# A recurrence with a mixer behind it on one core: another scan, mixer steps kept in PSUM, other buffers, and the order of all work written out as a list

## The chip, the cores and the metric

The kernel runs as one launch on one core of a Trainium2 chip. The metric is device microseconds (us) from start to end. The median of three runs of the kernel before is 1073.24 us (1073.01 to 1075.44). The profile is that of one further execution, read by engine: TensorE (PE, its weight loads PEld), VectorE (DVE), ScalarE (ACT), GpSimd (POOL), and SyncE (SP), which issues the DMAs.

## The reference

Two parts follow each other. The first is a linear recurrence over 768 tokens, for 4 batches x 8 heads with a state of 40 x 40:

```python
for t in range(S):                                   # S = 768
    y[:, :, t] = einsum('bhd,bhde->bhe', rt, state)
    Sa = einsum('bhde,bhe->bhd', state, at)
    state = state * wt[:, :, None, :] - einsum('bhd,bhe->bhde', Sa, bt) + einsum('bhd,bhe->bhde', vt, kt)
```

Its output, as rows of 320 values for each token, goes through a mixer:

```python
gate = 1 / (1 + exp(-gate_pre))                      # gate_pre: 5 taps of a causal convolution over tokens
x = (gate * (x @ w_val)) @ w_out                     # 320 x 320 each
xk, xr = mu_k*x + (1-mu_k)*x_prev, mu_r*x + (1-mu_r)*x_prev
k = maximum(xk @ w_k, 0);  v = (k*k) @ w_v           # 320 x 1024, 1024 x 320
out = 1 / (1 + exp(-(xr @ w_r))) * v
```

## The kernel before, in words

**The recurrence** (class `Attn`) goes through 24 chunks of 32 tokens. The decays are made into running products by scans on DVE, forward (`fwd`, L281) and backward (`bwd`, L294). The reciprocal of a chunk's total product (L284) times the forward products gives `ys` (POOL, L288). PE multiplies the scaled vectors among themselves (`gram`, L322), DVE masks the result (`gmask`, L326), and it is written to a scratch array in DRAM and read back with the 32 x 32 triangles of the (batch, head) pairs over all partitions. There the triangles are inverted, row after row, on DVE (`inv`, L368, L373, L376): in seven waves of chunks, (0,1), (2,3), (4 to 7), and so on; in the last five waves POOL takes rows 22 to 32 of each. The inverses go through DRAM to the layout `tr` of the steps.

The step of a chunk is a chain through the state: `yi` (PE, L443) reads the state `s0`; `gmm` (L458), `umm` (L471) and `fmm` (L492) follow, with a copy on ACT behind each of `yi`, `gmm` and `umm` and a masking on POOL (`cut`, L484); then `scl` (DVE, L501) scales the new state, `trn` turns it round on PE (L515, a transpose, and L516, a matmul with the identity, eight times each) and `trc` (ACT, L519) copies it to `s0` for the next chunk. The 32 pairs are handled as two groups, `gr` 0 and 1, so one block of `trn` stands for one chunk and one group: 46 blocks. The loads `wa`, `zt` and `vrt` of a step have one buffer each.

**The mixer** (class `Moe`) runs in 12 units of 64 tokens of each batch, 256 columns; unit u can begin when chunk 2u+1 is written out. Its steps are: load `X`; five taps on DVE (`tap`, L1007 the first, L1009 the others); sigmoid; the split of an operand into a high part (ACT, L805) and a low part (POOL, L809 and L811); the matmuls `val`, `out`, `k` (all in `fm`, L831), `r` (L883) and `v` (`vmm`, L891), three products for each pair of parts; and behind the `k` matmul `kpost`: relu (L870), which reads PSUM and frees its bank, square (L872), the high part (L874) and the low part (DVE, L876). The steps between matmuls lie in SBUF.

**PSUM** has eight banks, four for the recurrence (`pa`) and four for the mixer (`pm`). A task that begins a result takes a bank, and the last task that reads it gives it back.

**What sets the order.** Everything is a task with an engine, a cost, the tasks it needs, and a target time. `Plan.order` plays the tasks against a model of the engines and gives each engine its order; the kernel is then issued in it. Each engine works off its instructions strictly in that order.

The weights come as 64-bit words and are turned into two parts by seven small steps for each piece (`wconv`, L739 to L753).

Of the kernel before, what the change touches and what calls it, by code (L numbers as in the profile page):

```python
# [18 lines left out]
L = 32  # L19
# [29 lines left out]
F32_MIN_HI = 3.4332275390625e-05
PACE = 1.12  # L50
BURST = 3
ACC = [535.94, 4640.39]
GAP = 2.23
LAT = 170.0
DMA_RATE = 330.0
WAIT = {"p": 107.21, "v": 0, "a": 449.76, "g": 84.62, "d": 0.0}
WINDOW = 4096 / 1.2
COLUMNS = {"gram": 160, "ztr": 200, "rv": 160, "yi": 320, "gmm": 864, "umm": 288, "fmm": 1152, "trn": 200,
           "val": 2048, "out": 2048, "kmm": 2048, "rmm": 2560, "vmm": 1920}
WARM = 3072  # L60
# [14 lines left out]
class Task:  # L75
    def __init__(self, eng, cost, fn, deps, prio, bank, frees, nbytes, seq):
        self.eng, self.cost, self.fn, self.deps, self.prio = eng, cost, fn, deps, prio
        self.bank, self.frees, self.nbytes, self.seq = bank, frees, nbytes, seq
        self.left, self.ready, self.users = 0, 0.0, []


class Plan:
    """Puts the work of all engines in order by a model of their times: a task starts when the
    tasks it names are over and its engine is free; the one with the lowest priority number first."""

    def __init__(self):
        self.tasks, self.names, self.held, self.log = {}, set(), {}, []

    def add(self, name, eng, cost, fn, deps=(), prio=0.0, bank=None, frees=None, nbytes=0):
        assert name not in self.tasks, name  # L90
        prio += SHIFT.get(name[0], 0.0)
        self.tasks[name] = Task(eng, cost, fn, list(deps), prio, bank, frees, nbytes, len(self.tasks))
        self.names.add(name[0])

    def order(self):
# [1001 lines left out]
```

## Time and profile before

| | us |
|---|---|
| median of three runs | 1073.24 |
| the profiled execution, span | 1072.7 |
| PE busy in it | 823.6 (77%) |
| DVE busy | 610.5 (57%) |
| ACT busy | 465.3 (43%) |
| POOL busy | 375.1 (35%) |

Three stages can be told apart. Up to 294.0 us the first chunks are prepared and the weights converted, until the first `vmm` of unit 0 runs (at 293.50). From 294.0 to 981.0 recurrence and mixer run side by side; it ends when the last `fmm` does. From 981.0 to the end only the mixer is left. Busy times are sums of durations on one engine. The granted clock is the share of its full speed that TensorE was allowed; here it stands at 1.00 or at 0.50, and an average between the two means a mix of both.

### The profile page before, as it was taken

How to read it: one execution, taken by the hardware profiler on the slowest of the kernel's cores; microseconds unless marked ns; L12 is line 12 of the kernel's file. 1: busy time of each engine (PE TensorE's matmuls, PEld its weight loads, DVE VectorE, ACT ScalarE, POOL GpSimd, SP SyncE). 2: the span in 40 equal slices, each digit the busy share in tenths (PEclk: the TensorE clock that was granted, in tenths of full speed). 3: DMA queues.
4: the chain of work that ended last, by engine and by line, in shares of the span. 5: the costliest groups of instructions: out<-in, count | busy, mean ns of one | idle time of the engine just before them, and what ended most of it. 6: DMA issues, size and time to landing. Idle time of an engine off the chain costs nothing.

```text
span 1072.7 us, 33076 instructions
## 1 busy us (share of the span) xinstructions
PE 823.6 (77%) x14096; PEld 699.6 (65%) x14096; DVE 610.5 (57%) x1331; ACT 465.3 (43%) x1185; POOL 375.1 (35%) x477
## 2 busy tenths in 40 slices
PE   3222213864798868997998998796989999999998
PEld 2122112644676757887777877585868888889998
DVE  6546847837934783347686347855258525125662
ACT  6312213423523443354435532443355565456665
POOL 3433533334513442245331434323033123024431
PEclk9999999856768676588677775776878898679999
DMA  5453443551236314354135452234431433211101
GB/s 164 143 153 135 145 113 114 161 128 62 64 79 143 97 51 125 81 113 121 49 78 136 119 128 81 77 106 103 94 83 50 120 76 90 63 50 39 27 13 25
DMA packets 145903, 101.82 MB, mean 95 GB/s; under 512 B 120156, under 2 KB 123228, under 8 KB 143868
## 3 DMA queue, kind: packets, MB, share of 16 engines
q1 hardware_dynamic: 145756, 99.70, 35.1%
q8 instruction: 111, 1.82, 0.7%
q14 instruction: 36, 0.29, 0.1%
HBM read 66.64 MB, written 33.03 MB: 93 GB/s over the span
## 4 chain that ended last, share of the span: by engine, by line
PE 47%; DMA 20%; DVE 19%; SPq 6%; issue 3%; ACT 3%; POOL 1%; DVEq 0%; POOLq 0%; ACTq 0%
PE pm L831 13%; PE pa L516 7%; PE pm L891 7%; DMA d<-in_fd_dram 6%; SPq L246 6%; PE pa L515 5%; PE pa L492 4%; PE pa L443 3%; DMA X<-xs 3%; DVE tn L376 3%; DMA buf<-in_w_k_dram 3%; DVE buf L1009 3%; DVE tmv L373 3%; PE pm L883 2%; PE pa L458 2%
## 5 line engine op out<-in xcount | busy, mean ns | idle before, releaser
L484 POOL TENSOR_TENSOR mt<-mt,mask 64x512 f32<-64x512 f32 x48 | 65.1, 1358 | 154.0 <-ACT mt L479 44.1
L515 PE MATMUL pa<-ident,mt 40*40 40x40 f32 x368 | 83.6, 227 | 38.7 <-DVE sg L326 12.9
L516 PE MATMUL pa<-ident,mt 40*40 40x40 f32 x736 | 111.0, 241 | 0.4
L335 PE MATMUL pa<-ident,d 104*128 104x104 f32 x192 | 36.3, 334 | 94.7 <-POOL d L307 42.5
L492 PE MATMUL pa<-mt,zt 128*40 128x72 f32 x1536 | 78.1, 265 | 26.2 <-POOL mt L484 13.1
L831 PE MATMUL pm<-hh,whk 128*128 128x256 f32 x288 | 94.1, 332 | 1.7 <-POOL hh L811 1.3
L376 DVE TENSOR_TENSOR tn<-tn,tmv 128x240 f32<-128x240 f32 (+22 forms) x204 | 91.4, 448 | 4.5
L373 DVE TENSOR_TENSOR tmv<-tn,al 128x240 f32<-128x240 f32 (+22 forms) x204 | 89.7, 440 | 4.6
L335 PEld LDWEIGHTS pa<-ident,d 104*128 104x128 f32 x192 | 25.6, 185 | 100.5 <-POOL d L307 59.2
L492 PEld LDWEIGHTS pa<-mt,zt 128*40 128x40 f32 x1536 | 64.9, 141 | 36.3 <-POOL mt L484 15.4
L501 DVE TENSOR_TENSOR mt<-pa,cl 40x160 f32<-40x160 f32 x184 | 58.8, 319 | 51.1 <-PE pa L492 40.9
L831 PE MATMUL pm<-hh,wlk 128*128 128x256 f32 x288 | 87.2, 308 | 0.0
L479 ACT COPY mt<-pa 32x288 f32<-32x288 f32 x192 | 74.8, 390 | 27.9 <-PE pa L471 22.9
L307 POOL TENSOR_TENSOR d<-d,tl 104x512 f32<-104x512 f32 x42 | 62.7, 1499 | 56.1 <-DVE tl L294 39.3
L515 PEld LDWEIGHTS pa<-ident,mt 40*40 40x40 f32 x368 | 36.3, 99 | 65.7 <-DVE sg L326 13.7
L516 PEld LDWEIGHTS pa<-ident,mt 40*40 40x40 f32 x736 | 63.1, 128 | 22.7 <-DVE mt L501 1.1
L519 ACT COPY s<-pa 104x320 f32<-104x320 f32 x46 | 19.6, 426 | 132.2 <-PE pa L516 121.8
L876 DVE TENSOR_TENSOR kl<-buf,kh 128x512 fp32r<-128x512 f32 x48 | 37.5, 780 | 67.5 <-ACT kh L874 67.4
L322 PE MATMUL pa<-ya,d 40*32 40x32 f32 x3072 | 48.1, 223 | 32.8 <-ACT sz L339 11.5
L891 PE MATMUL pm<-whv,kh 128*128 128x320 f32 x192 | 72.4, 377 | 0.5 <-DVE buf L935 0.5
L322 PEld LDWEIGHTS pa<-ya,d 40*32 40x32 f32 x3072 | 41.0, 135 | 42.2 <-issue 15.3
L891 PE MATMUL pm<-whv,kl 128*128 128x320 f32 x192 | 65.8, 343 | 1.1 <-DVE kl L876 1.0
(128 smaller groups left out, 2175.8 us busy)
## 6 DMA issues: line engine op xcount, KB each, us to landing
d<-in_fd_dram SPq DMA_DIRECT2D x46, 322.8 KB
vrt<-in_vr_dram SPq DMA_DIRECT2D x48, 160.0 KB
slya<-ya SPq DMA_DIRECT2D x48, 160.0 KB
slab<-sz SPq DMA_DIRECT2D x24, 320.0 KB
zt<-slab SPq DMA_DIRECT2D x24, 320.0 KB
slab<-sg SPq DMA_DIRECT2D x24, 256.0 KB
mt<-in_vt_dram SPq DMA_DIRECT2D x48, 80.0 KB
ysj<-slya SPq DMA_DIRECT2D x48, 80.0 KB
```

The costliest lines, as they stand in the source:

```text
L246: self.nc.sync.dma_start(out, in_)
L307: e.tensor_mul(kb, kb, t3.unsqueeze(2).to_broadcast([104, 8, 2, L]))
L322: self.nc.tensor.matmul(ps[32 * q:32 * q + 32, i * L:(i + 1) * L], lhsT=kb[r:r + 40, m, o:o + L], rhs=ah[r:r + 40, m, :], start=True, stop ...
L373: eng.tensor_mul(t3, tn[:, lo:hi, k:k + 1].to_broadcast([128, ns, nt]), al[:, k:k + 1, k + 1:L].to_broadcast([128, ns, nt]))
L376: eng.tensor_add(tn[:, lo:hi, k + 1:L], tn[:, lo:hi, k + 1:L], t3)
L479: self.nc.scalar.copy(self.mv(gr)[96:128, 4 * mh:4 * mh + 4, par, :], ps[32 * q:32 * q + 32, 0:288].rearrange("p (m x) -> p m x", x=72))
L484: self.nc.gpsimd.tensor_mul(mm, mm, self.mask[64:128].unsqueeze(1).to_broadcast([64, 16, L]))
L492: self.nc.tensor.matmul(ps[r:r + 40, k * 72:k * 72 + 72], lhsT=self.zt[:, zof(mof(gr, i)) + par, :], rhs=self.mt[gr][:, 2 * i + par, :], s ...
L515: self.nc.tensor.transpose(ps[0:40, n], x[:, 0], one)
L516: self.nc.tensor.matmul(ps[64:104, n], lhsT=x[:, 1], rhs=one, start=True, stop=True)
L831: self.nc.tensor.matmul(ps[0:n, (mt % 2) * NT:(mt % 2) * NT + NT], lhsT=ww[:, mt * 128:mt * 128 + n], rhs=xx, start=(i == 0), stop=(i == l ...
L891: self.nc.tensor.matmul(ps[:, 0:DM], lhsT=xx[:, k, sl], rhs=ww, start=(k == 0 and i == 0), stop=(k == 7 and i == 2))
```

## The change

- **Seeded scan.** The backward scan comes first. The reciprocal of its totals is written into `seed`, and the forward scan starts from it, so that it gives `ys` at once: the POOL multiplication (L288) and the DVE copy of the totals (L285) go, and a small copy on ACT (`clc`) comes.
- **Mixer steps in PSUM.** The taps are added up in a PSUM bank, the first of them on ACT; the gate's product goes back into `val`'s bank, and its low part is taken on DVE from there; `mixadd` reads `out`'s bank; relu and square work in place in `k`'s bank until the low part has been read. The bits of the weight conversion lie in a PSUM bank too, its low part moves from POOL to DVE, and it has four buffers instead of three.
- **Scratch.** One array of 64 x 2304 for each chunk becomes two of 128 rows, `slg` and `slz`. The padding rows of `d` are set once by memsets instead of DMAs.
- **Inverses.** The rows of waves 0 and 1 are issued in blocks of eight, with one other DVE instruction among those of wave 0; all rows of the later waves are on DVE.
- **Double buffers** for `wa`, `zt` and `vrt`: a load waits for the step two chunks back.
- **trn** has no transpose any more: sixteen matmuls with the identity for a block.
- **Order.** `Plan.run` plays a fixed list of 3362 task numbers and a list of banks; there is no model in the kernel.

The diff, cut to what is spoken of (line numbers of the code after are given with the rows of its order below):

```diff
@@ Plan
+        order = [int(i) for line in ORDER for i in line.split()]
+        for i in order:
+            t = self.tasks[names[i]]
+            if t.bank and t.bank not in self.held:
+                self.held[t.bank] = int(next(banks))
+            t.fn()
...
@@ Attn: preparation
-    def fwd(self, c):
-        nc, n = self.nc, NM * (L + 1) + 1
-        nc.vector.tensor_tensor_scan(
-            self.ct[:, 0:n], self.d[c % 2][:, 0:n], self.rst[:, 0:n], 0.0, ALU.mult, ALU.add)
-        cl = self.cl[c % 12]
-        nc.vector.reciprocal(cl[:, 1, :], self.ct3()[:, :, L])
-        nc.vector.tensor_copy(cl[:, 0, :], self.ct3()[:, :, L])
-    def ys(self, c):
-        self.nc.gpsimd.tensor_mul(
...
+        nc.vector.reciprocal(self.seed[:, 0:YS:L + 1], self.total())
+    def clc(self, c):
+        self.nc.scalar.copy(self.cl[c % 12], self.total())
+    def fwd(self, c):
+        self.nc.vector.tensor_tensor_scan(self.ya[c % 2][:, 0:YS], self.d[c % 2][:, 0:YS], self.seed, 0.0,
+                                          ALU.mult, ALU.add)
...
@@ Attn: inverses
-SPLIT = [(("v", 0, 16),), (("v", 0, 16),)] + [(("v", 0, 22), ("g", 22, 32))] * 5
+SPLIT = [(("v", 0, 16),), (("v", 0, 16),)] + [(("v", 0, 32),)] * 5
+BLOCK = [8, 8] + [1] * 5
...
@@ Attn: step
-            [(n, c - 1, g) for n in ("rv", "yi") for g in range(2)], b - 0.9, nbytes=328e3)
+            [(n, c - 2, g) for n in ("rv", "yi") for g in range(2)], b - 0.9)
...
     def trn(self, c, gr):
         ps = self.bank("trn", c, gr)
         for i in range(8):
             x, n, one = self.mt[gr][0:40, 2 * i:2 * i + 2, 0:40], slice(i * D, i * D + D), self.ident[0:40, 0:40]
-            self.nc.tensor.transpose(ps[0:40, n], x[:, 0], one)
-            self.nc.tensor.matmul(ps[64:104, n], lhsT=x[:, 1], rhs=one, start=True, stop=True)
+            for par in range(2):
+                self.nc.tensor.matmul(ps[64 * par:64 * par + 40, n], lhsT=x[:, par], rhs=one, start=True, stop=True)
...
@@ Moe
-            nc.gpsimd.tensor_sub(p[4][0:n], bf[0:n], p[3][0:n])
+            nc.vector.tensor_sub(p[4], bf, p[3])
...
-        kr = self.kr[j % 2]
+        kr = self.bank("k", u, j).rearrange("p (k n) -> p k n", n=NT)
         if step == 0:
-            nc.scalar.activation(kr, self.bank("k", u, j).rearrange("p (k n) -> p k n", n=NT), AF.Relu)
+            nc.scalar.activation(kr, kr, AF.Relu)
...
-                add(("tap", u, k, t), "v", 396 if t else 266, lambda k=k, t=t: self.tapf(gt, k, t),
+                add(("tap", u, k, t), "v" if t else "a", 400 if t else 300, lambda k=k, t=t: self.tapf(u, k, t),
...
-            nc.vector.tensor_mul(gflat()[0:n, k], gflat()[0:n, k],
-                                 ps[0:n, 0:(2 - h) * NT].rearrange("p (k n) -> p k n", n=NT))
+            nc.vector.tensor_mul(ps, gflat()[0:n, k], ps)
...
+ORDER = [
...
+    "0 1826 7 487 6 27 3 1824 900 1841 1849 8 868 10 13 9 1833 12 1827 864 21 28 23 29 24 1842 11 5 31 19 33 34 30 16",
...
+]
```

Where the first step of the recurrence stands on PE before (the step of chunk 0, group 0; `mt` with the lower number is group 0, `x8` folds equal neighbours):

```order
L471 MATMUL pa_126<-gs_115,tr 32x72 x16
L322 MATMUL pa_124<-ya_103,d_87 32x32 x16
L471 MATMUL pa_126<-gs_116,tr 32x72 x16
L492 MATMUL pa_124<-mt_111,zt 40x72 x8
L492 MATMUL pa_126<-mt_111,zt 40x72 x8
L322 MATMUL pa_124<-ya_103,d_87 32x32 x16
L515 MATMUL pa_123<-ident,mt_111 40x40
L516 MATMUL pa_123<-ident,mt_111 40x40
L515 MATMUL pa_123<-ident,mt_111 40x40
L516 MATMUL pa_123<-ident,mt_111 40x40
```

The transpose L515 and the matmul L516 take turns, eight times each. The same place on PE now (L384 is `umm`, L405 `fmm`, L429 `trn`, L356 the `yi` of the next chunk):

```order
L384 MATMUL pa_132<-gs_123,tr 32x72 x16
L384 MATMUL pa_132<-gs_124,tr 32x72 x16
L405 MATMUL pa_132<-mt_119,zt_117 40x72 x16
L405 MATMUL pa_135<-mt_120,zt_117 40x72 x8
L429 MATMUL pa_132<-ident,mt_119 40x40 x16
L405 MATMUL pa_135<-mt_120,zt_117 40x72 x8
L356 MATMUL pa_132<-vrt_128,s_121 40x32 x16
L429 MATMUL pa_135<-ident,mt_120 40x40 x16
```

`trn` is one run of sixteen matmuls now. On DVE, among the inverses of wave 0, before (L373 and L376 are the inverse, L742 to L748 the weight conversion):

```order
L742 TENSOR_SCALAR buf<-buf 128x256
L373 TENSOR_TENSOR tmv<-tn,al 128x133
L744 SCALAR_TENSOR_TENSOR buf<-buf 128x256
L376 TENSOR_TENSOR tn<-tn,tmv 128x7x19
L746 SCALAR_TENSOR_TENSOR buf<-buf 128x256
L373 TENSOR_TENSOR tmv<-tn,al 128x126
L748 SCALAR_TENSOR_TENSOR buf<-buf 128x256
L376 TENSOR_TENSOR tn<-tn,tmv 128x7x18
```

61 other instructions of DVE lie among the 58 of wave 0, which end at DVE's 188th. Wave 0 on DVE now (L278, L283 and L286 are the inverse, L234 is `gmask`):

```order
L234 TENSOR_TENSOR sg<-pa_135,gm 128x2x128
L278 SCALAR_TENSOR_TENSOR tn<-al,tn 128x31
L278 SCALAR_TENSOR_TENSOR tn<-al,tn 128x30
L278 SCALAR_TENSOR_TENSOR tn<-al,tn 128x29 x2
L278 SCALAR_TENSOR_TENSOR tn<-al,tn 128x28 x2
L283 TENSOR_TENSOR tmv<-tn,al 128x81
L286 TENSOR_TENSOR tn<-tn,tmv 128x3x27
L283 TENSOR_TENSOR tmv<-tn,al 128x78
L286 TENSOR_TENSOR tn<-tn,tmv 128x3x26
```

The 58 have one other among them and end at DVE's 119th. Of the whole of DVE, 414 instructions stood ahead of the first low part of `kpost` (L876) before, and 476 stand there now; DVE has 1333 against 1345 in all, POOL 482 against 302. On PE, around the last `fmm` of the recurrence, before:

```order
L831 MATMUL pm_221<-hh_212,whval 128x256
L831 MATMUL pm_221<-hh_212,wlval 128x256
L492 MATMUL pa_126<-mt_112,zt 40x72 x8
L492 MATMUL pa_124<-mt_112,zt 40x72 x8
L831 MATMUL pm_219<-hh_212,whval 64x256
L831 MATMUL pm_219<-hh_212,wlval 64x256
L831 MATMUL pm_219<-hl_213,whval 64x256
```

It stands among `val` matmuls of the mixer, with 640 mixer matmuls behind it. Now:

```order
L820 MATMUL pm_255<-whv,kh 128x320
L405 MATMUL pa_132<-mt_119,zt_118 40x72 x8
L405 MATMUL pa_135<-mt_119,zt_118 40x72 x8
L405 MATMUL pa_134<-mt_120,zt_118 40x72 x8
L405 MATMUL pa_133<-mt_120,zt_118 40x72 x8
L820 MATMUL pm_255<-whv,kh 128x320
L820 MATMUL pm_255<-wlv,kh 128x320
```

It stands among `vmm` matmuls (L820), and 504 mixer matmuls are behind it. The matmuls of PE are 8386 in both.

## Rows read from the trace of the kernel before

**Rows 1.** Stretches: window, its length, busy of PE, PEld, DVE, ACT, POOL; clock, DMA.
```profile
0.00:283.50 283.50, 112.35 (x2648) 92.03 (x2648) 190.15 (x413) 93.47 (x229) 116.20 (x136) 0.90 0.44 128
0.00:294.00 294.00, 118.69 (x2754) 96.87 (x2755) 199.53 (x434) 99.17 (x243) 118.85 (x137) 0.89 0.43 125
294.00:981.00 687.00, 620.16 (x10705) 519.65 (x10703) 366.92 (x820) 311.25 (x821) 226.39 (x296) 0.75 0.36 91
981.00:1072.70 91.70, 84.75 (x643) 83.12 (x640) 44.09 (x78) 54.85 (x122) 29.84 (x45) 1.00 0.10 24
```

**Rows 2.** The page's chain that ended last, share by engine.
```profile
PE 47%; DMA 20%; DVE 19%; SPq 6%; issue 3%; ACT 3%; POOL 1%; DVEq 0%; POOLq 0%; ACTq 0%
```

**Rows 3.** Stretches, line L515 alone: window, length, busy of PE, PEld; clock, DMA.
```profile
294.00:981.00 687.00, 73.68 (x328) 32.09 (x328) 0.75 0.36 91
```

**Rows 4.** Timeline of PE, 854 to 864: start us, us, engine, line, operation, tiles.
```profile
853.77 1.20 PE L492 MATMUL pa<-mt,zt 128*40 128x72 f32 x32
854.90 0.80 PE L443 MATMUL pa<-vrt,s 40*40 40x32 f32 x32
855.63 0.39 PE L831 MATMUL pm<-hh,whk 128*128 128x256 f32 x1
...
856.78 0.21 PE L515 MATMUL pa<-ident,mt 40*40 40x40 f32 x1
856.92 0.27 PE L516 MATMUL pa<-ident,mt 40*40 40x40 f32 x2
...
859.47 0.71 PE L458 MATMUL pa<-mt,wa 96*32 96x72 f32 x32
```

**Rows 5.** Timeline of PE, 287 to 298.
```profile
287.69 0.25 PE L515 MATMUL pa<-ident,mt 40*40 40x40 f32 x1 [4.15 <-ACT mt L435]
...
291.38 1.19 PE L492 MATMUL pa<-mt,zt 128*40 128x72 f32 x16
...
295.40 1.28 PE L443 MATMUL pa<-vrt,s 40*40 40x32 f32 x32
296.61 0.63 PE L891 MATMUL pm<-whv,kh 128*128 128x320 f32 x1
```

**Rows 6.** Stretches around those matmuls, columns as in Rows 1.
```profile
854.90:859.45 4.55, 4.55 (x68) 3.64 (x64) 2.08 (x6) 3.35 (x8) 0.00 (x0) 1.00 0.62 155
859.45:863.35 3.90, 3.90 (x50) 3.60 (x48) 0.06 (x1) 0.73 (x2) 0.00 (x0) 0.65 0.02 6
287.70:296.20 8.50, 8.50 (x134) 6.70 (x136) 7.35 (x22) 3.88 (x9) 0.00 (x0) 0.50 0.32 80
```

**Rows 7.** Timeline of DVE, 62 to 136: first and last of wave 0.
```profile
62.25 1.30 DVE L368 SCALAR_TENSOR_TENSOR tn<-al,tn 128x31 f32<-128x31 f32 x6 [0.86 <-DMA al<-slab]
...
135.07 0.18 DVE L376 TENSOR_TENSOR tn<-tn,tmv 128x16 f32<-128x16 f32 x1
```

**Rows 8.** Groups by line: out<-in, count | busy, mean ns | idle before, releasers.
```profile
L872 ACT ACTIVATE buf<-buf 128x512 f32<-128x512 f32 x48 | 30.3, 631 | 1.5
L874 ACT CAST kh<-buf 128x512 fp32r<-128x512 f32 x48 | 29.7, 620 | 1.5
L876 DVE TENSOR_TENSOR kl<-buf,kh 128x512 fp32r<-128x512 f32 x48 | 37.5, 780 | 67.5 <-ACT kh L874 67.4
L285 DVE COPY cl<-ct 104x16 f32<-104x16 f32 x24 | 12.8, 535 | 0.0
L376 POOL TENSOR_TENSOR tn<-tn,tmg 128x9 f32<-128x9 f32 (+4 forms) x45 | 13.1, 291 | 3.4
L373 POOL TENSOR_TENSOR tmg<-tn,al 128x9 f32<-128x9 f32 (+4 forms) x45 | 12.2, 272 | 63.9 <-DMA al<-slab 38.5 <-DMA X<-xs 22.4
```

**Rows 9.** Timeline of DVE, 720 to 737: taps of one unit.
```profile
725.61 0.35 DVE L1007 TENSOR_SCALAR f<-X,cw 128x256 f32<-128x256 f32 x1 [2.33 <-DMA X<-xs]
...
726.82 6.62 DVE L1009 SCALAR_TENSOR_TENSOR f<-X,cw,f 128x256 f32<-128x256 f32 x7
```

**Rows 10.** Waits: who waited for whom, us in total, times, longest.
```profile
PE pa L427 <- DMA vrt<-in_vr_dram: 17.5, 8, 10.6
```

More of the change, by code (lines that the diff above doesn't have):

```diff
@@ L49 @@
-F32_MIN_HI = 3.4332275390625e-05
[L50 to L60, printed above, removed]
+INV_PRIO = [[-13.59, -21.51], [-16.35, -2.92], [-9.58, 3.45], [1.16, 10.77], [12.69, 1.13], [-27.43, -5.02], [45.44,
+            33.25]]
@@ L75, with __init__ @@
 class Task:
[L76 to L79, printed above, removed]
+    def __init__(self, fn, deps, bank, frees):
+        self.fn, self.deps, self.bank, self.frees = fn, deps, bank, frees
 class Plan:
     def __init__(self):
-        self.tasks, self.names, self.held, self.log = {}, set(), {}, []
@@ L89, in add @@
-    def add(self, name, eng, cost, fn, deps=(), prio=0.0, bank=None, frees=None, nbytes=0):
+        self.tasks, self.held = {}, {}
+    def add(self, name, eng, cost, fn, deps=(), prio=0.0, bank=None, frees=None):
         assert name not in self.tasks, name
[L91 to L95, printed above, removed]
-        T, held = self.tasks, {}
-        engines = "pvagd"
-        free = {e: 0.0 for e in engines}
-        todo = {e: [] for e in engines}
-        banks = {k: [(0.0, i) for i in range(4)] for k in "am"}
-        holds = {}
-        for n, t in T.items():
-            t.name = n
-            for d in t.deps:
-                assert d[0] in self.names, (n, d)
-                if d in T:
-                    t.left += 1
-                    T[d].users.append(t)
+        self.tasks[name] = Task(fn, deps, bank, frees)
@@ new lines, in run @@
+        order = [int(i) for line in ORDER for i in line.split()]
+        assert sorted(order) == list(range(len(names)))
+        for i in order:
+            t = self.tasks[names[i]]
+            assert all(d in done for d in t.deps if d in self.tasks), names[i]
+            if t.bank and t.bank not in self.held:
+                self.held[t.bank] = int(next(banks))
+                assert users.setdefault((t.bank[0], self.held[t.bank]), t.bank) == t.bank, names[i]
+            t.fn()
+            done.add(names[i])
@@ L178, in order, with __init__ @@
                 if not holds[t.frees]:
[L179 to L192 removed]
+                    users.pop((t.frees[0], self.held[t.frees]))
 class Attn:
[L196 removed]
+    def __init__(self, ctx, tc, plan, fd, vr, vt, xs):
         self.nc, self.plan = tc.nc, plan
[L198 removed]
+        self.fd, self.vr, self.vt, self.xs = fd, vr, vt, xs
         nc = self.nc
```

544 lines of the change are left out of this document (244 added, 300 removed), and 141 rows, old and new, of the table ORDER.

## The prediction

> **What bounds the kernel now.** I read the stretches by stage first, then the chain that ended last, then TensorE's timeline where the clock differs, then DVE's timeline in the first stage. The stretches [rows 1] show three stages with different limits. In the first (to 294.0 us) no engine is full: PE is busy 118.7 us, DVE 199.5. DVE comes closest, but up to 283.5 us, when the first low part of `kpost` runs, 283.5 - 190.2 = 93 us of it are idle: it waits for results and loads. In the second stage (687.0 us) PE is busy 620.2 us, 90%, and its granted clock is 0.75. In the third (91.7 us) only the mixer is left, PE is busy 84.8 us and the clock is 1.00. So PE bounds 779 us of the span, and in 687 of them it runs at less than full clock. The chain [rows 2] agrees: PE has 47% of it, DMA 20% and DVE 19%, the latter two mostly early.
>
> The clock has two levels, 1.2 and 2.4 GHz, shown as 0.50 and 1.00 [rows 6]. A mean of 0.75 is half of the time at each. The timeline around 857 us [rows 4, 6] shows a fall: the clock is 1.00 from 854.90 to 859.45, a stretch that ends with a `trn` block, and 0.65 in the 3.90 us behind it. In those the mixer's matmuls follow each other without a gap.
>
> **The change part by part.** The profiled span is 1072.7 us, 0.5 below the median of the runs; the sum goes against the span and the 0.5 is added at the end.
>
> *trn.* At full clock a block of 8 transposes and 8 matmuls goes from 856.78 to 859.47: 2.69 us [rows 4]. At half clock one goes from 287.69 to 291.38: 3.69 us [rows 5]. What takes its place is 16 plain float32 matmuls, 32 records. The nearest row is `yi`, which has 32 records of 32 columns in 854.90 to 855.63, 0.73 us [rows 4], and at half clock in 295.40 to 296.61, 1.21 us [rows 5]. `trn` has 40 columns: 0.73 x 40/32 = 0.91 us and 1.21 x 40/32 = 1.51 us. One block saves 1.78 at full clock and 2.18 at half. Line L515 has 328 transposes in the second stage [rows 3], 8 for each block: 41 blocks, half of the time at either level: 41 x 1.98 = 81 us. Bounds: at `yi`'s own time 41 x (1.96 + 2.48)/2 = 91; at the time of `fmm`, with its 72 columns (853.77 to 854.90, 1.13 us [rows 4]; 1.13 x 1.21/0.73 = 1.87 at half), 41 x (1.56 + 1.82)/2 = 69. That the sixteen cost as much as now, 0, is a rival below. I take 81, since `yi` has the same records with nearly the same columns. The five blocks of the first stage stand where PE waits, and count nothing.
>
> *The clock in the second stage.* PE's other work there is 620 - 41 x (2.69 + 3.69)/2 = 620 - 131 = 489 us at 0.75. The row on the fall [rows 6] has a `trn` block just ahead. If blocks a third as long let the clock fall less often, it ends between the rows I have: 0.75 in this stage, 1.00 in the last [rows 1]. The first stage, with many gaps, had 0.89. I take 0.90: 489 x 0.75/0.90 = 408, a gain of 81 us. Bounds: 0 (it stays) and 489 x 0.25 = 122 (full throughout).
>
> The Trainium skill has a rule on this ("TensorE: Matmul & The Clock Gate", section "🔬 Part 4: PE-mode transpose"): full clock doesn't engage for transpose mode, which doesn't count as PE being busy in the same way. The trace agrees as far as it goes, with the 0.65 behind the block; by that rule alone the clock would be 1.00 now, and this term 122.
>
> *First stage.* Up to the first low part of `kpost` DVE has 476 instructions now, 414 before. At the mean of that stretch, 190.15/413 = 0.46 us [rows 1], the 62 more are +28 us if all lie on the path. Against it, wave 0 of the inverses took from 62.25 to 135.07, 72.9 us [rows 7], with 61 other instructions between; now it is 59 in a row, 59 x 0.46 = 27 us, so its end, on which the first step of the recurrence waits, comes up to 46 us earlier. Bounds +28 and -46; no row decides between them, and I take their middle, -10 us. Queued behind the block on DVE are the weight conversions, which the mixer needs only after the second chunk.
>
> *Last stage.* 640 mixer matmuls stood behind the last `fmm`, 504 now. At the same pace 504/640 x 91.7 [rows 1] = 72.2, a gain of 19.5 us. PE's work is the same in all, so this is a gain only if the 136 matmuls that move forward go into PE's idle time of the second stage, 687.0 - 620.2 = 67 us [rows 1]; at 91.7/640 = 0.143 us each they need 19.5. Bounds 0 and -19.5; I take -19.5.
>
> *What costs nothing.* The double buffers end a wait of PE for `vrt` of 17.5 us in all [rows 10], most of it early; what is late next is the state's own chain. If all of it were on the path, -17.5. The seeded scan takes the multiplication off POOL (35% busy in the span) and the copy L285, 12.8 us, off DVE [rows 8]. DVE gets POOL's share of the inverses, 12.2 + 13.1 = 25.3 us [rows 8], and 36 low parts of the gate at about 0.39 (half of L876's 0.780, which is twice as wide [rows 8]) = 14; it loses 36 first taps at 0.35 [rows 9] = 13 and the 12.8. Net +14 us, most of it in a stage where DVE is idle for 687 - 367 = 320 us. Without that cover: +14. The more and smaller DMAs of the new scratch lie beside a DMA share of 0.36 [rows 1].
>
> Sum: 1072.7 - 10 - 81 - 81 - 19.5 = 881.2, with the 0.5 about 882; I say 881. The second stage would then have 525 us.
>
> **The rivals.**
>
> (a) *The clock doesn't follow.* Then the sum is 881 + 81 = 962. For it: the clock also falls where I can't see the reason. Against it: the row of the fall. Range 930 to 1000.
>
> (b) *All goes well:* clock 1.00 (41 more), the first stage at its bound, 36 less: 881 - 41 - 36 = 804; range 776 (with the double buffers and yet more of PE's idle time) to 835.
>
> (c) *DVE becomes the bound of the second stage.* With PE faster, DVE must do its 367 + 14 us of work there in less time. In the first stretch, where everything waits for it, it reached a share of 190.2/283.5 = 0.67 [rows 1]. At 0.67 the second stage needs 381/0.67 = 569 us rather than 525: 925. At the 0.62 midway between 0.67 and the 0.57 of the whole span (the table) it needs 615: 971. `scl` stands on DVE between `fmm` and `trn`, so a queue there hits the state's chain. Against it: the order may put `scl` in front.
>
> (d) *Mixer banks held longer: slower.* `k`'s bank was free after the relu; now also after square, high part and low part: 0.631 + 0.620 + 0.780 = 2.03 us, 48 times [rows 8], 97 us. The taps now hold banks while 12 operations of 6.62/7 = 0.95 us [rows 9] run, 11.3 us a unit, 136 us in 12 units. If PE stood still in all of that, it would cost 233: 881 + 233 = 1114. It decides only if more than 192 of the 233 are exposed; with four banks for the mixer and the recurrence's matmuls to go in between, I think it unlikely.
>
> (e) *trn isn't cheaper.* A transpose takes 0.14 us before the change (856.78 to 856.92 [rows 4]). If plain matmuls needed four times as long as a transpose, a block would take 16 x 0.56 = 9.0 us instead of 2.69, at full clock +6.3 in 41 blocks = +258, on a sum without the two gains (1043): 1301. Against it: `yi`'s 32 records in 0.73 us [rows 4] are plain float32.
>
> The rule that speaks for (e) is in the Trainium skill ("TensorE: Matmul & The Clock Gate", section "Terms"): the transpose mode is four times faster for FP32. The trace of `yi` disagrees for operands this small.
>
> **How the numbers follow.** My forecast, 835 to 930, has 0.50; (b) 0.13; (a) 0.16; (c) beyond 930 0.12; (d) 0.06; (e) or the change not doing what it says 0.03. The first four are faster, as far as they stay below 1070: 0.91. Slower by over 0.3% (3 us, about what a measurement of this kernel can tell from no change): (d) and (e) without what falls within, 0.07. Within 0.3%: 0.02. The range that leaves out 0.2: 800 to 985; the likeliest case alone, 835 to 930.
>
> **What would show it.** In the profile after: `trn` blocks of about 0.9 us at clock 1.00 (2.7 would show the first term wrong); a granted clock of about 0.90 between the first `vmm` and the last `fmm` (0.75 shows (a)); the first low part of `kpost` near 273 us; wave 0 in about 27 us; 72 us behind the last `fmm`; DVE's share of the second stage under 0.75 and `trn` not waiting for `scl` (else (c)); relu or mixer matmuls waiting for banks only in small pieces (else (d)). The prediction is wrong above all if PE's clock stays where it is, or if the second stage isn't bound by PE once `trn` is short.

## The result

The changed kernel takes 768.24 us (754.90 to 783.55, 4 runs), 0.708 of before, 95% interval 0.702 to 0.713. Sent to the chip once more it took 767.22 (0.713, 0.709 to 0.717). The forecast, 881, and its range, 800 to 985, lay above it: the direction was right, the size far too small. The ratio leaves out the two longest of its runs, which have a lower clock; the profiled execution, with a span of 781.8 us, is one of them, and the second profile (772.4) is shown where that matters.

The chain that ended last, on the page of after:

```profile
PE 56%; DMA 14%; DVE 14%; issue 6%; ACT 5%; SPq 4%; POOL 1%; POOLq 0%; DVEq 0%; ACTq 0%
```

[Rows 2] gave DMA and SyncE's queue 26% of 1072.7, 279 us; here it is 18% of 781.8, 141 us. Of the 291 us by which the span is shorter, 138 have left these two shares.

The stages of after, cut at the first `vmm` and the last `fmm` (columns as in Rows 1), and the middle one from the second profile:

```profile
0.00:225.90 225.90, 122.47 (x3324) 105.79 (x3324) 185.67 (x487) 112.20 (x289) 61.62 (x71) 0.82 0.68 174
225.90:709.30 483.40, 450.11 (x10647) 403.78 (x10637) 317.42 (x792) 312.89 (x853) 162.84 (x195) 0.90 0.51 125
709.30:781.80 72.50, 66.79 (x506) 65.73 (x504) 30.82 (x66) 41.48 (x98) 17.80 (x33) 0.99 0.12 27
```
```profile
227.80:699.90 472.10, 437.83 (x10645) 392.15 (x10638) 319.85 (x792) 313.30 (x853) 162.81 (x195) 0.93 0.53 128
```

Against [rows 1] the first stage, which ends at the first `vmm` (293.5 before), is 67.6 us shorter (forecast 10), the second 204 (forecast 162), the third 19.2 (forecast 19.5). In the second stage PE's clock rose from 0.75 to 0.90 (0.93 in the second profile). PE's busy time there fell by 620.2 - 450.1 = 170 us, where the forecast's terms make 162 - 19.5 = 142.5, and its idle time fell from 67 to 33 us, where they leave 47.5. The first stage's DMA share is up from 0.43 to 0.68.

The parts that were priced, in the trace of after. `trn` at full and at half clock (TensorE's timeline at 388 and 254 us, and below it the stretch of the second, with the clock at 0.50):

```profile
388.46 0.81 PE L429 MATMUL pa<-ident,mt 40*40 40x40 f32 x32
389.20 0.39 PE L760 MATMUL pm<-hh,whk 128*128 128x256 f32 x1
```
```profile
254.21 1.29 PE L429 MATMUL pa<-ident,mt 40*40 40x40 f32 x32
255.43 1.19 PE L371 MATMUL pa<-mt,wa 96*32 96x72 f32 x32
```
```profile
254.21:255.43 1.22, 1.22 (x34) 1.14 (x33) 1.12 (x3) 0.00 (x0) 0.12 (x1) 0.50 0.05 15
```

0.74 and 1.22 us from start to start, against 2.69 and 3.69 [rows 4, 5]. Wave 0 of the inverses on DVE, first and last:

```profile
44.39 1.30 DVE L278 SCALAR_TENSOR_TENSOR tn<-al,tn 128x31 f32<-128x31 f32 x6 [1.87 <-DMA al<-slg]
...
61.75 0.19 DVE L286 TENSOR_TENSOR tn<-tn,tmv 128x16 f32<-128x16 f32 x1
```

It begins 17.9 us earlier than in [rows 7] and takes 17.6 us instead of 73. It begins when `al` has come back from the scratch; that start is the first sign of what follows.

### The profile page after: what moved, and what is told of

Same layout as the page of the kernel before. It is cut to its first block, busy times and chain, and to the rows that moved or that the text cites. A ratio compares the mean times of both kernels' runs of the same rounds, so it can differ in the third digit from the quotient of the medians.

```text
span 781.8 us, 33563 instructions
## 1 busy us (share of the span) xinstructions
PE 639.4 (82%) x14464; PEld 575.3 (74%) x14464; DVE 533.9 (68%) x1343; ACT 466.6 (60%) x1238; POOL 242.3 (31%) x297
## 4 chain that ended last, share of the span: by engine, by line
PE 56%; DMA 14%; DVE 14%; issue 6%; ACT 5%; SPq 4%; POOL 1%; POOLq 0%; DVEq 0%; ACTq 0%
PE pm L760 19%; PE pm L820 9%; PE pa L405 5%; DMA d<-in_fd_dram 4%; PE pa L356 4%; PE pa L384 3%; SPq L156 3%; PE pa L429 3%; PE pa L371 3%; PE pm L812 3%; PE pa L230 3%; DVE mt L414 2%; PE pa L243 2%; DMA X<-xs 2%; PE pa L340 2%
## 5 line engine op out<-in xcount | busy, mean ns | idle before, releaser
L405 PE MATMUL pa<-mt,zt 128*40 128x72 f32 x1536 | 71.0, 248 | 18.7 <-DVE mt L414 5.0
L940 DVE SCALAR_TENSOR_TENSOR pm<-X,cw,pm 128x256 f32<-128x256 f32 (+1 forms) x144 | 67.4, 482 | 22.3 <-ACT pm L938 14.2
L283 DVE TENSOR_TENSOR tmv<-tn,al 128x112 f32<-128x112 f32 (+18 forms) x204 | 75.8, 372 | 5.0
L405 PEld LDWEIGHTS pa<-mt,zt 128*40 128x40 f32 x1536 | 58.2, 129 | 28.4 <-issue 8.7
L286 DVE TENSOR_TENSOR tn<-tn,tmv 128x112 f32<-128x112 f32 (+18 forms) x204 | 73.4, 360 | 5.0
L820 PE MATMUL pm<-whv,kh 128*128 128x320 f32 x192 | 66.2, 345 | 1.2 <-DVE buf L923 1.2
L348 ACT COPY mt<-pa 32x128 f32<-32x128 f32 x192 | 49.0, 255 | 29.9 <-PE pa L405 15.7
L760 PEld LDWEIGHTS pm<-hh,whk 128*128 128x128 f32 x288 | 59.0, 205 | 5.6 <-ACT buf L851 2.1
L805 DVE TENSOR_TENSOR kl<-pm,kh 128x512 fp32r<-128x512 f32 x48 | 32.4, 683 | 43.4 <-ACT kh L803 43.3
L820 PE MATMUL pm<-wlv,kh 128*128 128x320 f32 x192 | 61.3, 319 | 0.0
L820 PE MATMUL pm<-whv,kl 128*128 128x320 f32 x192 | 61.3, 319 | 0.0
L760 PEld LDWEIGHTS pm<-hh,wlk 128*128 128x128 f32 x288 | 59.3, 206 | 0.0
L760 PE MATMUL pm<-hl,whk 128*128 128x256 f32 x192 | 57.2, 298 | 0.2 <-POOL hl L735 0.2
L384 PE MATMUL pa<-gs,tr 32*32 32x72 f32 x1536 | 41.2, 250 | 16.8 <-DMA tr<-td 11.9
```

The lines of the kernel that those rows point to most:

```text
L283: eng.tensor_mul(t3, tn[:, lo:hi, k:k + 1].to_broadcast([128, ns, nt]), al[:, k:k + 1, k + 1:L].to_broadcast([128, ns, nt]))
L286: eng.tensor_add(tn[:, lo:hi, k + 1:L], tn[:, lo:hi, k + 1:L], t3)
L384: self.nc.tensor.matmul(ps[32 * q:32 * q + 32, sl], lhsT=self.tr[32 * q:32 * q + 32, c % WCH, gr * 4 + i % 4, :], rhs=g[32 * q:32 * q + 32 ...
L405: self.nc.tensor.matmul(ps[r:r + 40, k * 72:k * 72 + 72], lhsT=self.zt[c % 2][:, zof(mof(gr, i)) + par, :], rhs=self.mt[gr][:, 2 * i + par ...
L760: self.nc.tensor.matmul(ps[0:n, (mt % 2) * NT:(mt % 2) * NT + NT], lhsT=ww[:, mt * 128:mt * 128 + n], rhs=xx, start=(i == 0), stop=(i == l ...
L820: self.nc.tensor.matmul(ps[:, 0:DM], lhsT=xx[:, k, sl], rhs=ww, start=(k == 0 and i == 0), stop=(k == 7 and i == 2))
```

## The experiments

Below, "gaps" in an expectation are stretches of PE beyond the usual distance from one task to the next; in the text idle is the length of a stretch less PE's busy time. The second stage runs from the first `vmm` to the last `fmm`.

**1. The new trn alone, in the kernel before.**

```diff
-            self.nc.tensor.transpose(ps[0:40, n], x[:, 0], one)
-            self.nc.tensor.matmul(ps[64:104, n], lhsT=x[:, 1], rhs=one, start=True, stop=True)
+            for par in range(2):
+                self.nc.tensor.matmul(ps[64 * par:64 * par + 40, n], lhsT=x[:, par], rhs=one, start=True, stop=True)
```

> The kernel before with the new trn alone (two matmuls in place of transpose and matmul; order of all engines unchanged). Theory A (trn and the clock are most of the gain of the second stage, as predicted): trn takes 0.74 us at full and 1.22 us at half clock, as after; 41 blocks save 41 x (1.95 + 2.47)/2 = 91 us, and the clock of the second stage rises from 0.75 towards 0.90: between 900 and 985 us. Theory B (the new order and the buffers brought it, and what trn frees is given back as waits): the time stays above 1030 us, with more PE idle time in the second stage. Clock between 294 us and the last fmm: A 0.85 to 0.92, B 0.75.

982.32 us, ratio 0.916 (0.910 to 0.923). Its second stage:

```profile
292.50:888.30 595.80, 487.06 (x11037) 425.31 (x11034) 365.30 (x822) 310.47 (x821) 230.71 (x296) 0.82 0.42 106
```

PE is busy 133 us less than before and the clock is 0.82, but PE now idles 109 us instead of 67. Theory A holds for the blocks and half for the clock; part came back as waits.

**2. The old trn, in the changed kernel** (the same edit the other way round).

> The changed kernel with the old trn (transpose and matmul), all else as it is. Theory A: +91 us for the blocks alone and the clock falls back towards 0.75: 860 to 945 us. Theory B: the new order has room for it: 768 to 800 us.

914.27 us, ratio 0.852 (0.844 to 0.859): 147 us more than the changed kernel took beside the later runs (767.22, run 9). The second stage:

```profile
236.00:839.10 603.10, 583.02 (x10346) 498.30 (x10334) 312.66 (x792) 314.00 (x853) 161.75 (x196) 0.78 0.40 100
```

PE idles 20 us only: there is nothing to hide trn behind. Theory A holds.

**3. Plain matmuls for as long as the old trn.**

```diff
-            for par in range(2):
+            for par in (0, 1) * 3:
```

> The changed kernel with each of the sixteen matmuls of trn issued three times (same result): a block takes about 2.2 us at full clock and 3.7 at half, nearly the old length, but with no transpose in it. If it is the transposes that let the clock fall: the clock stays at 0.88 or above and the time is 768 + 46 x 1.6 = about 842 us at most. If it is small matmuls of any kind, or the length of the block: the clock falls as in the run with the old trn, and the time is within 20 us of that run.

838.25 us, ratio 0.781 (0.774 to 0.787), and the clock of the second stage is 0.92, as in after. A block takes 1.96 us at full clock, a little less than expected and 0.73 of the old block's 2.69. So neither small matmuls nor a block of this length lower the clock. Run 10 shows that it isn't the transposes as such either.

**4. Waves 0 and 1 in one run each, in the kernel before.**

```diff
+BLOCK = [31, 31] + [1] * 5
...
+                    if BLOCK[w] > 1:
+                        todo = [(("inv", w, k, part, "b"), cost, block)]
```

> The kernel before with the DVE instructions of waves 0 and 1 of the inverses issued in one run per wave, the planner putting everything else around them as it does. Theory C (the first stage is set by the chain through wave 0, which took 72.9 us before and 17.4 after): the first umm comes 45 to 55 us earlier than at 165 us and the time falls by 30 to 58 us, to 1015 to 1043. Theory D (the first stage is set by other work of DVE, the weights and the masks): the first umm comes earlier, but the first low part of kpost stays within 10 us of 283.5, and the time within 15 us of 1073.

1061.64 us, ratio 0.988 (0.979 to 0.998). The first `umm` comes at 103.4 us instead of 165.4, the first `vmm` at 275.1 instead of 293.5, and 12 us are left in the end. Between the theories, nearer to D: 62 us at the first `umm` are worth 18 in the stage.

**5. The planner of before on the tasks of after.**

```diff
-        order = [int(i) for line in ORDER for i in line.split()]
+        self.order()
+        for s, fin, e, t, warm, b in self.log:
```

> The changed kernel's tasks, targets and buffers, but put in order by the planner of before (its model and rule, without its corrections by kind, and with rv made to wait for umm of the chunk before, since the planner else runs out of PSUM banks) in place of the list. Theory L (the list is what fills PE's waits: 143 us of PE gaps in the second stage in the kernel before with the new trn, 62 in the changed one): the gaps come back to over 110 us and the time is above 840 us. Theory P (buffers, engines and PSUM fill them): within 40 us of 768. The planner's model of times wasn't made for these tasks, so a slow run tells less than a fast one.

887.68 us, ratio 0.829 (0.825 to 0.833). The second stage:

```profile
231.30:831.40 600.10, 494.49 (x11057) 443.63 (x11055) 366.27 (x854) 326.96 (x879) 192.94 (x210) 0.83 0.41 106
```

PE idles 106 us, and the clock is 0.83. The first stage is as short as with the list. Theory L for the second stage; since that planner wasn't fitted to these tasks, 120 us is an upper bound for the list.

**6. Wave 0 spread again, in the changed kernel.**

```diff
+            for i, n in enumerate(inv):
+                if i:
+                    pos[n] = pos[rest[61 * i // len(inv)]] + 0.5
```

> The changed kernel with the four blocks of wave 0 on DVE spread among the 61 DVE instructions that follow them in its order (about what before had between them); order of the other engines as it is, but for what must come later. Theory C (wave 0's chain sets the first stage): the first umm comes 20 to 30 us later than 74 us, the first vmm 15 to 30 later than 226, the time 10 to 30 us longer. Theory D (other work sets it): first umm later by the same, first vmm and time within 8 us.

795.52 us, ratio 0.743 (0.739 to 0.748): 28 us longer, first `umm` at 96.0 and first `vmm` at 244.8. Theory C holds. The first stage is 17 to 19 us longer than in the two profiles of after, which agrees with the 18 of run 4; what the block is worth in the whole time differs, 28 us here and 12 there.

**7. One buffer each for wa, zt and vrt, in the changed kernel.**

```diff
-        self.wa = [T(f"wa{i}", [128, 2, NM, L]) for i in range(2)]
+        self.wa = [T("wa", [128, 2, NM, L])] * 2
...
-            [(n, c - 2, g) for n in ("rv", "yi") for g in range(2)], b - 0.9)
+            [(n, c - 1, g) for n in ("rv", "yi") for g in range(2)], b - 0.9)
```

> The changed kernel with one buffer each for wa, zt and vrt: their loads wait for the step of the chunk before. The DMA issues and a few matmuls move behind in the order, the rest stays. As the prediction has it (they cost and bring nothing): within 10 us of 768. Rival (they are part of what filled PE's waits): PE's gaps in the second stage rise from 62 by 30 us or more and the time by 25 to 80 us.

802.43 us, ratio 0.745 (0.740 to 0.751): some 35 us longer. The profiled execution is 19 us longer than the second profile of after (791.6 against 772.4); 16.5 of them are in the second stage, where PE idles 48 us instead of 34. The rival holds for the time; the idle time rose by 14 us, where 30 in gaps were expected.

**8. The other transposes as matmuls.**

```diff
-            self.nc.tensor.transpose(ps[:, 128 * i:128 * i + 104], self.kb(c)[0:104, o:o + 128],
-                                     self.ident[0:104, 0:104])
+            self.nc.tensor.matmul(ps[:, 128 * i:128 * i + 104], lhsT=self.kb(c)[0:104, o:o + 128],
+                                  rhs=self.ident[0:104, 0:104], start=True, stop=True)
```

> The changed kernel with the transposes that are left (ztr, four for each of 48 blocks) made plain matmuls with the identity. If transposes are what lets the clock fall: the mean granted clock rises from 0.90 to 0.93 or above and the time falls by 8 to 25 us. If it falls for PE's idle time in the first 230 us and other reasons: clock and time stay (within 6 us), since eight records of 104 columns take about the 0.45 us that the four transposes took.

775.81 us, ratio 0.723 (0.719 to 0.726). The mean clock is 0.944 in the profiled execution, but 0.914 to 0.920 in the other three, where after has 0.888 to 0.922: no clear rise. A block of `ztr` takes 1.07 us from start to start instead of 0.60 (medians of 48, the second taken from the second profile of after), and the time doesn't fall. Here plain matmuls cost 1.8 times the transposes.

**9. The changed kernel once more.**

> The changed kernel once more, beside the others on the same chip, since its first runs lay between 755 and 784 us: 755 to 784 again, the longer ones at a lower mean granted clock (0.89 at 784, 0.92 at 755 in the first runs).

767.22 us (761.03 to 774.10). What follows is compared with this.

**10. The old operations of trn, but the transposes first and then the matmuls.**

```diff
+        for i in range(8):
+            self.nc.tensor.transpose(ps[0:40, i * D:i * D + D], x(i, 0), one)
+        for i in range(8):
+            self.nc.tensor.matmul(ps[64:104, i * D:i * D + D], lhsT=x(i, 1), rhs=one, start=True, stop=True)
```

> The changed kernel with the old operations of trn, but the eight transposes first and then the eight matmuls. If the turns between the two kinds made the old block slow: a block takes at most 1.0 us at full clock and the time is 765 to 790 us. If each transpose takes its 0.14 us: 8 x 0.14 + 8 x 0.046 = 1.5 us a block, +35 us in 46, and with some fall of the clock 800 to 840 us. If transposes let the clock fall however they are grouped, the mean clock is below 0.88.

771.30 us, ratio 0.715 (0.710 to 0.720), the same as after, and in the profile the clock of the second stage is the highest of all (the mean clock of its four executions is 0.917 to 0.953). A block on PE, and that stage:

```profile
389.76 0.46 PE L428 MATMUL pa<-ident,mt 40*40 40x40 f32 x8
390.15 0.80 PE L430 MATMUL pa<-ident,mt 40*40 40x40 f32 x16
390.88 0.39 PE L761 MATMUL pm<-hh,whk 128*128 128x256 f32 x1
```
```profile
224.40:694.30 469.90, 441.80 (x10345) 395.98 (x10333) 318.63 (x794) 313.50 (x853) 166.17 (x197) 0.96 0.52 129
```

Eight transposes in a row take 0.39 us, 0.05 each; taking turns with matmuls they took 0.14 [rows 4]. The eight matmuls take 0.73 us, 0.09 each; in the old block 2.69 - 8 x 0.14 leaves 0.20 for each. The block is 1.12 us instead of 2.69, a little above the 1.0 expected. What made `trn` long was the change between the two kinds, sixteen times a block. And with all its transposes the clock is 0.96: that transposes let it fall however they are grouped is refuted. The same operations taking turns had 0.78 (run 2).

**11 and 12. Half of the change each, under the planner of before:** the new recurrence with the old mixer, and the old recurrence with the new mixer. (Whole classes are exchanged, so no diff is shown.)

> The whole recurrence of the changed kernel (scan, scratch, blocks, double buffers, trn) with the mixer of before, in the order of the planner of before. Together with the next run it splits the 186 us by which the changed kernel's tasks are faster than before under that planner (1074 to 888). Theory: trn brings its 92 and the first stage 20 to 45 of it by the block and the seeded scan: 920 to 965 us, first vmm at 240 to 275 us. Rival: the mixer's part is what shortens the first stage: first vmm above 275 us.

> The mixer of the changed kernel (steps in PSUM, first tap on ACT, low parts on DVE, four weight buffers) with the recurrence of before, in the order of the planner of before. Theory (the mixer's part only helps where the recurrence isn't the bound): 1035 to 1080 us, first vmm above 275 us. Rival (it frees POOL and shortens the first stage): below 1035 us, first vmm below 265 us.

916.56 us, ratio 0.852 (0.847 to 0.857), first `vmm` at 235.0; and 1068.08 us, ratio 0.991 (0.987 to 0.995), first `vmm` at 297.6. Both theories hold, the first a little beyond its ranges (920 and 240): 58.5 of the first stage's 67.6 us come with the recurrence, and the mixer's part by itself brings under 1%.

**13. Blocks and double buffers, in the kernel before.**

```diff
-        self.vrt = T("vrt", [104, NM, 2, L])
+        self.vrt = [T(f"vrt{i}", [104, NM, 2, L]) for i in range(2)]
...
-            [(n, c - 1, g) for n in ("rv", "yi") for g in range(2)], b - 0.9, nbytes=328e3)
+            [(n, c - 2, g) for n in ("rv", "yi") for g in range(2)], b - 0.9, nbytes=328e3)
```

> The kernel before with waves 0 and 1 in one run each (as in the run with blocks alone) and two buffers each for wa, zt and vrt (rv waits for umm of the chunk before, so that the planner has banks). In the first stage SyncE's queue stood 30 us behind loads that wait for a step of the chunk before. If that is what kept the first stage long: first vmm 15 to 35 us earlier than the 275 us with blocks alone, and the time 15 to 40 us shorter than 1062. If the loads are not on the path: within 10 us of both.

1071.19 us, ratio 0.997 (0.994 to 1.001), first `vmm` at 280.7: no gain. The buffers are not what shortened the first stage; their worth in run 7 hangs on the rest.

**14. The old scratch, in the changed kernel.**

```diff
-        self.slg = [dp.tile([128, 512], F32, name=f"slg{c}") for c in range(NCH)]
-        self.slz = [dp.tile([128, 640], F32, name=f"slz{c}") for c in range(NCH)]
+        self.slab = [dp.tile([64, 2304], F32, name=f"slab{c}") for c in range(NCH)]
...
-        self.dma(dst[c], t[:, c % 2])
+        self.dma(self.slab[c][:, sl].rearrange("a (x y) -> x a y", x=2), t[:, c % 2])
```

> The changed kernel with the scratch of before (one array of 64 x 2304 for each chunk), the order as it is. If the new layout made the round trips of the first chunks shorter: first umm 5 us or more later than 74 to 77 us, first vmm 8 us or more later than 226 to 228, time 10 to 25 us longer than 767. If not: within 6 us.

914.27 us, ratio 0.851 (0.845 to 0.857): 147 us longer, as much as the old trn and far beyond the 10 to 25 expected. The first stage and the second:

```profile
0.00:288.60 288.60, 122.94 (x3324) 105.96 (x3324) 183.79 (x484) 111.94 (x288) 58.32 (x69) 0.81 0.48 135
288.60:839.30 550.70, 468.36 (x10645) 419.54 (x10637) 317.81 (x795) 314.07 (x854) 165.60 (x197) 0.85 0.43 110
```

61 us in the first stage (against the second profile of after); in the second PE idles 82 us instead of 34 and the clock is 0.85 instead of 0.93. SyncE's queue of this run and of after, around the second write of the scratch and the first read:

```profile
27.76 0.53 SPq L155 DMA_DIRECT2D slab<-sg  x1
32.05 5.26 SPq L155 DMA_DIRECT2D al<-slab  x2
```
```profile
27.19 0.35 SPq L156 DMA_DIRECT2D slg<-sg  x1
27.64 2.15 SPq L156 DMA_DIRECT2D al<-slg  x4
```

The write that `al` reads was issued at 19.9 us in both. In after SyncE issues the read at once, in run 14 it stands 3.8 us first, and everything queued behind stands with it. While it stands, the DMA engines do little (columns as in Rows 1):

```profile
29.00:31.50 2.50, 0.00 (x0) 0.00 (x0) 1.50 (x2) 0.53 (x3) 0.78 (x1) 1.00 0.13 52
```

The DMA share, second from the end, is the mean over 16 engines, and 0.13 of 16 is two. The traces also record how the semaphore that reports a DMA as landed is counted up, and they say the same. Each of the 48 writes counts it up in 3 steps with the old scratch, in before as in run 14, one about 1 us after the issue and two at the end; with the new one it is 16 steps (after, runs 17 and 18). The reads have 16 in all of them. From the issue to the last step a write of `sg` takes 8.8 us in before and 10.6 in run 14, against 4.0 in after and 2.9 in run 17 (medians of 24). Wave 0 on DVE, whose input comes back from there, begins at 55.0 us instead of 44.4:

```profile
55.00 1.30 DVE L275 SCALAR_TENSOR_TENSOR tn<-al,tn 128x31 f32<-128x31 f32 x6 [10.70 <-DMA al<-slab]
```

Over the run SyncE's own waits for these writes (us in total, times, longest) are, in run 14 and in after,

```profile
SPq L155 <- DMA slab<-sz: 21.6, 9, 5.6
...
SPq L155 <- DMA slab<-sg: 16.3, 7, 6.1
```
```profile
SPq L156 <- DMA slg<-sg: 1.5, 2, 1.1
```

and after has none for `slz<-sz`. Summed over all rows of the view of waits that end in a DMA, the engines wait 397 us in before, 103 in after and 308 here.

**15. The forward scan without its seed.**

```diff
+        self.nc.gpsimd.tensor_mul(ys, ys, self.seed[:, 0:YS:L + 1].unsqueeze(2).to_broadcast([PX, NM, L]))
```

> The changed kernel with the forward scan unseeded and the reciprocal of the total multiplied in on POOL behind it, as before (24 multiplications of about 1.2 us; the copy of the totals stays on ACT). As the prediction has it (off the path): within 8 us of 767. Rival (it stands in the chain of the first chunks and on POOL ahead of cut): first vmm 5 us later or more, time 10 to 30 us longer.

773.74 us, ratio 0.722 (0.716 to 0.727), first `vmm` at 225.7: 6.5 us with overlapping intervals, off the path as forecast.

**16. The weights' loads issued by ScalarE.**

```diff
-            self.dma(t[p0:p0 + a.shape[0]], a.bitcast(I32))
+            self.nc.scalar.dma_start(t[p0:p0 + a.shape[0]], a.bitcast(I32))
```

> The changed kernel with the loads of the weights issued by ScalarE instead of SyncE, at the same places of the list. In its first stage SyncE waits 24 us for the buffers of the weights while other loads stand behind. If that queue sets the first stage: first vmm 5 to 15 us earlier, time 755 or less. If ACT, which now waits in its place, is worse: 5 to 30 us longer.

794.80 us, ratio 0.738 (0.732 to 0.745), first `vmm` at 245.8. ACT waits instead, and it is worse.

**17. The new scratch alone, in the kernel before** (the edit of run 14 the other way round).

> The kernel before with the two scratch arrays of 128 rows of the changed kernel, nothing else; the order of PE, DVE, ACT and POOL is the same. In the changed kernel the old scratch cost 147 us (914 against 767): 61 in the first stage, 79 in the second. If it costs as much in before: 925 to 960 us. If its price hangs on the rest (before is held by trn and by its order as well): 1000 to 1060 us, with less time in which engines wait for DMAs (397 us in before, by the sum of the waits). If it costs nothing there: above 1065.

995.46 us, ratio 0.924 (0.917 to 0.930). The first two stages:

```profile
0.00:238.30 238.30, 119.86 (x2753) 97.44 (x2753) 205.21 (x433) 98.86 (x243) 121.00 (x137) 0.95 0.60 154
238.30:900.80 662.50, 612.95 (x10709) 515.41 (x10706) 366.84 (x822) 309.55 (x821) 228.19 (x296) 0.76 0.38 95
```

The time is just below the second range: the price hangs on the rest. The first stage is 55 us shorter with nothing else changed, the second 25. The engines' waits that end in a DMA fall from 397 to 152 us. SyncE's queue in before and in this run, at the same place:

```profile
40.69 12.38 SPq L246 DMA_DIRECT2D al<-slab  x2
```
```profile
36.60 3.42 SPq L247 DMA_DIRECT2D al<-slg  x4
```

12.4 us for two reads became 3.4 for four.

**18. Both parts in one array, with rows as in the changed kernel.**

```diff
+        self.sl = [dp.tile([128, 1152], F32, name=f"sl{c}") for c in range(NCH)]
+        self.slg, self.slz = [t[:, 0:512] for t in self.sl], [t[:, 512:1152] for t in self.sl]
```

> The changed kernel with both scratch parts in one array of 128 x 1152 for each chunk (rows as in the changed kernel, in one array as before). If it is the shape of the rows (each write of 128 whole rows, in place of two halves of 64) that makes the round trips short: 755 to 785 us. If it is that reads of one part wait for writes of the other: above 850 us, with waits of SyncE for sl<-sz and sl<-sg of 30 us or more.

772.29 us (760.70 to 776.47), within the spread of after. One array or two doesn't matter: it is the shape in which a write is given to the DMA. The reads changed along with the writes, and no run changes the writes alone; but the reads have 16 steps either way, and those of `al` take 5.1 us to land in before and 5.9 in run 14, 4.4 in after and 4.3 in run 17 (medians).

That shape stands in the code (the diff of run 14): with `rearrange("a (x y) -> x a y", x=2)` the DRAM side of a write of `sg` is 2 x 64 x 512, without it 128 x 512. Both move 128 rows of 2 KB. The Trainium skill ("DMA: Bandwidth & Descriptors", section "🔬 Why a DMA increments its semaphore by 16 and not by 1") says that a DMA is spread over the largest number of engines, at most 16, that divides the slowest dimension of both sides: 2 for the first form, 16 for the second. The trace agrees: 0.13 of 16 engines is two, and the steps at the end of a write are two with the first form; with the second form there are 16 steps.

No version beat the changed kernel by more than its spread: the grouped trn (771) and the single array (772) equal it.

## Why the prediction was wrong

**The step that failed** is the last sentence of "What costs nothing": "The more and smaller DMAs of the new scratch lie beside a DMA share of 0.36." They are the largest part of the change beside trn: 79 us alone in before (run 17), 147 when taken out of after (run 14). The step asked whether the DMAs have bandwidth to spare. (The 0.36 is the second stage's; the first has 0.43 [rows 1].) The question was how long a round trip takes and what stands behind it on SyncE: a write of `sg` takes 8.8 us to land in before and 4.0 in after. The profile had it: DMA and SyncE's queue hold 26% of the chain [rows 2], of which the prediction read out DMA's 20% and gave them no price. Of the 99 us by which the profiled span lies below the sum (881.2 - 781.8), 58 are in the first stage and 42 in the second; the last is as forecast.

**First stage, -10 with bounds +28 and -46 (their middle is -9); it was -67.6.** The failed step again: 55 of it come with the scratch alone (run 17). The block of wave 0 was put at up to 46 us earlier; in this stage it is worth 17 to 19 us (runs 4 and 6). The +28 didn't appear: DVE has more instructions in the stage and is yet busy 185.7 us instead of 199.5 [rows 1].

**trn, -81.** Right, and at its bound of 91: 0.74 and 1.22 us instead of the 0.91 and 1.51 taken. Rival (e) is out. These are 10 of the 28 us by which PE's busy time in the second stage fell further than the terms make; the rest was not separated. Part of it goes with work that moved forward: PE has 3324 records in the first stage, 2754 before [rows 1].

**The clock, 0.75 to 0.90.** The size was right, the reason not. The prediction laid it on the length of the blocks; blocks of 1.96 us leave the clock at 0.92 (run 3). What lowered it is that transposes and matmuls took turns: 0.78 with the old trn (run 2), 0.96 with the same operations grouped (run 10). The new trn alone gives 0.82 (run 1). The rest goes with PE's idle time, which is 109 us there, 106 in run 5 (0.83), 82 in run 14 (0.85) and 33 in after; that the idle time is its cause is not shown by itself. The rule of the Trainium skill that was weighed there ("TensorE: Matmul & The Clock Gate", section "🔬 Part 4: PE-mode transpose") is not what acts here: run 10 keeps the transposes and has 0.96.

**PE's idle time in the second stage,** which the sum left as it was, 67 us less the 19.5 that the last stage's matmuls fill. By itself the new trn raises it to 109 (run 1): the waits that trn had hidden come out. It is 33 in after, since the scratch (48 us, run 14), the list (up to 72, run 5) and the buffers (14, run 7) each take some away; these overlap and don't add up.

**The last stage, -19.5.** Right: 19.2.

**Rivals.** (a) didn't come, the clock rose. (c), DVE as the bound, didn't come: its share of the second stage is 317.4/483.4 = 0.66, and its work there fell from 366.9 to 317.4 us, where +14 was forecast. (d) didn't come: PE idles 33 us in the whole stage. (b) was nearest in its mechanism, PE's idle time gone and the first stage short, but its bound of 776 was still above the result, since it held the first stage at -46; its clock of 1.00 didn't come.

Still open are how the worth of the list and that of the buffers split where they meet, and why the first stage of after, with the scratch, wave 0 and the list, gains 68 us where the scratch alone gives 55.

## What to carry to other kernels

Price a changed DMA by its round trip and by what waits behind it on the issuing queue, not by the mean DMA share; look at its dimensions as they are given to the DMA, the slowest above all, and at the DMA share of the chain. A part can be worth more when it is taken out of the full version (trn and scratch, 147 us each) than when it is put into the old one (92 and 79): one wait hides another. Keep operations of a kind together on TensorE.

## What the runs showed of the hardware that was not expected

A transpose of 40 x 40 takes 0.05 us among transposes and 0.14 between matmuls (run 10, [rows 4]). Eight matmuls that all write rows 64 to 104 of the bank take 0.73 us (run 10), and sixteen that write rows 0 to 40 and 64 to 104 in turn take 0.74 (after); why was not tried.

Taps on DVE are longer while a POOL operation runs beside them. The second to fifth taps, in before (SBUF; the 72 shown go to `f`, 72 more to `buf`) and in after (PSUM); the columns are the count, and least, median and longest ns:

```profile
L1009 DVE SCALAR_TENSOR_TENSOR f<-X,cw,f x72: 452/474/1554, 239.5 to 1012.9; 128x256 f32<-128x256 f32 x48, 64x256 f32<-64x256 f32 x24
```
```profile
L940 DVE SCALAR_TENSOR_TENSOR pm<-X,cw,pm x144: 410/481/492, 147.4 to 741.9; 128x256 f32<-128x256 f32 x96, 64x256 f32<-64x256 f32 x48
```

In before, the 79 taps that had a POOL operation beside them for over half of their time took 778 ns on the mean, the 63 without one 471. In PSUM none takes over 492. That it is POOL was seen in these records and not tried by itself. DVE's busy time fell from 610.5 to 533.9 us in all; how much of that comes from this was not separated.
